# Three edits in the first MLP of an attention-and-two-MLPs kernel: when v is asked for, when tail rows are stored, and the order in which shared fused products are split

## The chip, the cores and the metric

The kernel runs on one core of one Trainium2 chip. The metric is device time in microseconds (us) of one execution. The kernel before takes 1601.68 us, the median of three runs (1598.41 to 1603.44).

## The reference, cut to what matters

A packed attention (32 packing queries p for each of 64 heads) feeds two MLPs. All inputs and outputs are float32.

```python
def sm_attn(qq, kk, vv):
    s = scale * np.matmul(qq, kk.transpose(0, 1, 3, 2))
    s = s - np.max(s, axis=-1, keepdims=True)
    a = np.exp(s)
    a = a / (np.sum(a, axis=-1, keepdims=True) + 1e-09)
    return np.matmul(a, vv)
p_packed = sm_attn(p, k, v)                # batch 8, heads 8, 576 positions, head size 64; p: 32 rows
out = sm_attn(q, p_packed, p_packed)
x = out.transpose(0, 2, 1, 3).reshape(4608, 512)
h = x @ w_in;  x = (h * (1 / (1 + np.exp(-h)))) @ w_out          # first MLP: 512 -> 2048 -> 512
h = x @ w_in2; y = (h * np.clip(h + 3, 0, 6) / 6) @ w_out2       # second MLP, the same sizes
```

## The kernel before

**Tiling.** Sixteen attention groups (batch and four heads each, called n) are worked through in windows that run beside the first MLP. The first MLP has nine blocks j of 512 tokens; blocks 1 to 7 each take the 512 head rows of one batch, block 8 the 64 tail rows of all batches. In each block a loop over 16 slices f of the hidden layer forms `hidden` (lines 829 to 831), applies Silu, splits the result into a high and a low part (`split_g`, lines 844 and 845), and `project` (lines 852 to 854) adds the slice to four PSUM accumulators. Every float32 product is three matmuls over high and low parts: high by high, high by low, low by high. The second MLP follows from about 850 us on and is not touched.

**Fused products.** In blocks 1 to 7 the packed values are multiplied into `w_in` first (`fuse_steps`, lines 617 to 619), so that `hidden` needs only the attention weights. Blocks 2 and 3, 4 and 5, 6 and 7 are mates: one product of 128 rows holds 64 rows for the one and 64 rows for the other (`two`). Each product lies in one PSUM bank; `split` copies its high part on ACT (line 623) and subtracts on DVE for the low part (line 624), for 64 rows at a time when there are mates. There are 48 such shared products: three pairs, four column groups g, two head groups qd, two halves j. The bank comes from a pool of four, which `hidden` also draws on, and it is free again after the last low part. The first mate's tiles are called `fused` in the trace, the second mate's `xf`, `raw`, `xh` and `xl`, by the buffer that they borrow.

**The order.** `window` writes the attention steps of a window in a fixed order with their needs; `Plan` runs them between the MLP's matmuls when their needs have been met for so many steps (`WAIT`, counted in matmul triples). `step_pp` multiplies the attention weights by v (lines 459 to 462); `step_pt` transposes the packed values (line 479). `step_xt` copies a tail result (line 105, tile `xt`), and `flush` stores it (line 562).

**The queue.** Nearly all transfers of the first MLP are issued by SP in program order, and an issue that waits holds all behind it. `load_next` issues the next v, q or k of a list (`uses`), up to three uses ahead. A v load overwrites `vt`, the only buffer for v's tail rows (line 325), so it waits for the matmuls of `step_pp` that read the one before (line 462). On the same queue stand the fused weights' loads `wi` (line 222), `wo` (line 235), and the stores of `Prep` (lines 309 to 311): `Prep` converts the second MLP's weights in one buffer `c`, which POOL (line 293) fills again only after its last store has landed; DVE (lines 296 to 299) then works on it.

Of the kernel before, what the change touches and what calls it, by code (L numbers as in the profile page):

```python
# [18 lines left out]
def tile_pack_attention_two_mlps(ctx: ExitStack, tc, q, k, v, p, w_in1, w_out1, w_in2, w_out2, out):  # L19
# [8 lines left out]
    nc = tc.nc  # L28
# [4 lines left out]
    P = 128  # L33
# [47 lines left out]
    f32 = lambda ap: ap.bitcast(F32)  # L81
# [8 lines left out]
    def bank():  # L90

        pool, tag = (ps_h, "h")
        if early[0]:
            pool, tag = banks[0]
            banks.append(banks.pop(0))
        return pool.tile([P, T], F32, tag=tag, name="abank")
# [4 lines left out]
    def copy(out, in_):  # L101
        (nc.vector.tensor_copy if other[0] else nc.scalar.copy)(out=out, in_=in_)
# [253 lines left out]
    def pair(t, pr):  # L356
        return t[:, 2 * pr:2 * pr + 2, :].rearrange("p h d -> p (h d)")
# [94 lines left out]
    def step_pp(n):  # L452
        vm, vt = [nat.pop(("v", n, j)) for j in range(2)], nat.pop(("v", n))
        a, at_ = st.pop(("a1", n)), st.pop(("a1t", n))
        r = st.pop(("r1", n))
        ps = bank()
        for i in range(NI):
            for h in range(HQ):
                mm(ps[h * NP:(h + 1) * NP, 0:D], lhsT=a[:, i * P + h * NP:i * P + (h + 1) * NP], rhs=vm[h // 2][:, h % 2, i, :],
                   start=i == 0, stop=False)  # L460
        for h in range(HQ):
            mm(ps[h * NP:(h + 1) * NP, 0:D], lhsT=at_[:, h * NP:(h + 1) * NP], rhs=vt[:, h, :], start=False, stop=True)
        pf = at.tile([P, HQ, D], F32, tag="ppf", name="ppf", bufs=3)
        pn = at.tile([P, 1, D], F32, tag="ppn", name="ppn")
        nc.vector.tensor_scalar(out=pn[:, 0, :], in0=ps[:, 0:D], scalar1=r[:, 1:2], scalar2=None, op0=ALU.mult)
        nc.vector.tensor_tensor(out=pf, in0=pn.to_broadcast([P, HQ, D]), in1=mask.to_broadcast([P, HQ, D]), op=ALU.mult)
        st["pp", n] = pf
        if early[0]:
            ph = at.tile([P, HQ, D], F32R, tag="ph", name="ph", bufs=2)
            pl = at.tile([P, HQ, D], F32R, tag="pl", name="pl", bufs=2)  # L470
            copy(out=ph, in_=pf)
            nc.gpsimd.tensor_sub(out=pl, in0=pf, in1=f32(ph))
            st["ps", n] = ph, pl

    def step_pt(n):
        pf = st["pp", n]
        ps = bank()
        for j in range(2):
            nc.tensor.transpose(ps[:, j * P:(j + 1) * P], pair(pf, j), ident)
        t = at.tile([P, 2 * P], F32, tag="ppT", name="ppT", bufs=4)  # L480
        copy_short(out=t, in_=ps[:, 0:2 * P])
        st["ppT", n] = t
# [96 lines left out]
    fused = {}  # L579
# [28 lines left out]
    def fuse_steps(b, g):  # L608

        ms = mates[b]  # L610
        steps = []

        def product(ps, j, qd, first, last):
            lh, ll = [t[:, j * P:(j + 1) * P] for t in st["lp", b, qd]]
            w = have_in[b, g, 2 * qd + j]
            rh, rl = w[:, 0], w[:, 1]
            mm(ps, lhsT=lh, rhs=rh, start=first, stop=False)
            mm(ps, lhsT=lh, rhs=rl, start=False, stop=False)
            mm(ps, lhsT=ll, rhs=rh, start=False, stop=last)

        def split(dst, ps, rows):
            hi, lo = dst[0][rows, :], dst[1][rows, :]
            nc.scalar.copy(out=hi, in_=ps[rows, :])
            nc.vector.tensor_sub(out=lo, in0=ps[rows, :], in1=f32(hi))  # L624

        def one(qd):
            ps = bank()
            for j in range(2):
                product(ps, j, qd, j == 0, j == 1)
            fused[b, g, qd] = fused_tiles(b, g, qd)  # L630
            split(fused[b, g, qd], ps, slice(0, P))
            next_in()
            next_in()

        def two(qd, j):
            ps = bank()
            product(ps, j, qd, True, True)
            for m, bm in enumerate(ms):
                if j == 0:
                    fused[bm, g, qd] = fused_tiles(bm, g, qd)  # L640
                o = m * 64 if j == 0 else (1 - m) * 64
                split(fused[bm, g, qd], ps, slice(o, o + 64))
            next_in()

        for qd in range(QPB):
            if len(ms) == 1:
                steps.append(lambda qd=qd: one(qd))
            else:
                for j in range(2):
                    steps.append(lambda qd=qd, j=j: two(qd, j))  # L650
        return steps
# [9 lines left out]
    uses = []  # L661
# [7 lines left out]
    loaded, used = [0], set()  # L669
    cs = [c for ws in WINDOWS for c, _ in ws if c is not None]  # L670

    def load_next():

        while loaded[0] < len(uses) and (loaded[0] < AHEAD or uses[loaded[0] - AHEAD] in used):
            what, n = uses[loaded[0]]
            loaded[0] += 1
            if what != "k":
                load_tail(n, what)
            for j in range(2):
                load_nat(n, what, j)  # L680

    def use(what, n):
        used.add((what, n))
        load_next()
# [8 lines left out]
    class Plan:  # L693
# [11 lines left out]
        def add(self, key, place, cost, fn, need=(), tile=None, bank=0):  # L705
            self.steps.append((place, key, cost, fn, need, tile, bank))
            self.open.add(key)
# [46 lines left out]
    def window(c, d, b, a):  # L754


        steps = []

        before = ("exps", b, a), ("ends", b, a)

        def add(n, what, cost, fn, *need, tile=None, bank=5):
            if n is not None:
                steps.append(((what, n), cost, fn, need, tile, bank))

        def exps():
            for n, fn in (c, exp1), (d, exp2):
                if n is not None:
                    fn(n)

        def ends():  # L770
            for n, fn in (c, post1), (d, post2):
                if n is not None:
                    fn(n)

        def kpq():
            step_kpq(c, d)
            if c is not None:
                load_p_after(c)

        add(c, "spread", 0, lambda: spread_p(c), ("kpq", b), bank=0)  # L780
        add(c if c is not None else d, "kpq", 3 if c is not None else 1, kpq, ("spread", c), ("st", b), ("zt", a))
        add(b, "t", 2, lambda: step_t(b), before[0], tile=("pp", b))
        add(d, "q0", 0, lambda: step_tr(d, "q", 0), bank=0, tile=("z", d))
        add(b, "tt", 1, lambda: step_tt(b), before[0])
        add(d, "q1", 0, lambda: [step_tr(d, "q", 1), use("q", d)], ("q0", d), bank=0, tile=("z", d))
        ends_block = a is not None and a % QPB == QPB - 1
        if ends_block:
            a = None
        add(a, "u", 0, lambda: [step_u(a), step_ut(a)], before[1], bank=8)
        add(b, "pp", 4, lambda: [step_pp(b), use("v", b)], ("t", b), ("tt", b))  # L790
        add(a, "xt", 1, lambda: step_xt(a), ("u", a))
        add(a, "flush", 0, flush, ("xt", a), bank=0)
        add(b, "pt", 1, lambda: step_pt(b), ("pp", b))
        add(d, "z", 4, lambda: step_z(d), ("pt", d), ("q0", d), ("q1", d), (("u", a), 0), bank=9)
        add(c, "k0", 0, lambda: step_tr(c, "k", 0), (("pp", b), 0), bank=0, tile=("s", c))
        add(d, "zt", 1, lambda: step_zt(d), ("z", d), ("kpq", c if c is not None else d))
        add(c, "k1", 0, lambda: [step_tr(c, "k", 1), use("k", c)], ("k0", c), bank=0, tile=("s", c))
        add(c, "s", 4, lambda: step_s(c), ("k1", c), ("kpq", c), ("tt", b))
        add(c, "st", 1, lambda: step_st(c), ("s", c))
        steps.append((("exps", c, d), 0, exps, (("st", c), ("zt", d)), None, 0))  # L800
        steps.append((("ends", c, d), 0, ends, (("exps", c, d),), None, 0))
        return steps

    WAIT = {"spread": 8, "kpq": 7, "q0": 6, "q1": 6, "k0": 6, "k1": 6, "t": 6, "tt": 5, "pp": 9, "pt": 6, "z": 4, "zt": 10, "s": 4, "st": 7,
            "exps": 18, "ends": 18, "u": 14, "split": 10}
    FIRST = {**WAIT, "ends": 16, "spread": 20, "exps": 14, "pt": 14, "tt": 8, "t": 8, "k1": 8}


# [122 lines left out]
    class Second:  # L931
# [212 lines left out]
        def split(self, s):  # L1144
            if s < FD * S7:
                self.split_hi(s)
                self.split_lo(s)
# [249 lines left out]
    for j in range(NBLK):  # L1397
# [16 lines left out]
        if j in mates:  # L1414
            for g in range(1, NG):
                fs = fuse_steps(j, g)
                lo, hi = [max(0, 18 * g * GF - 24) / (18 * NF) for g in (g - 1, g)]
                for i, fn in enumerate(fs):
                    plan.add(("m", j, g, i), lo + (hi - lo) * 0.7 * (i + 0.5) / len(fs), 6 if len(mates[j]) == 1 else 3, fn, bank=11)
        if j + 1 in mates:  # L1420
            lo = max(at_pp, (18 * 3 * GF - 24) / (18 * NF))
# [86 lines left out]
```

## Time and profile before

| | |
|---|---|
| median of three runs | 1601.68 us |
| the profiled execution, its own time | 1596.71 us |
| its span, first to last instruction | 1594.9 us |
| PE busy, share of the span | 97% |
| DVE, ACT, POOL busy | 65%, 51%, 12% |
| mean granted TensorE clock | 0.988 |

The table is of one profiled execution. PE is the busiest engine by far; the time that can be won is where PE stands idle, or runs at a lower granted clock, so idle time in front of a PE instruction is the first thing to look for, and what ended it the second.

### The profile page before, as it was taken

How to read it: one execution, taken by the hardware profiler on the slowest of the kernel's cores; microseconds unless marked ns; L12 is line 12 of the kernel's file. 1: busy time of each engine (PE TensorE's matmuls, PEld its weight loads, DVE VectorE, ACT ScalarE, POOL GpSimd, SP SyncE). 2: the span in 40 equal slices, each digit the busy share in tenths (PEclk: the TensorE clock that was granted, in tenths of full speed). 3: DMA queues.
4: the chain of work that ended last, by engine and by line, in shares of the span. 5: the costliest groups of instructions: out<-in, count | busy, mean ns of one | idle time of the engine just before them, and what ended most of it. 6: DMA issues, size and time to landing. Idle time of an engine off the chain costs nothing.

```text
span 1594.9 us, 23740 instructions
## 1 busy us (share of the span) xinstructions
PE 1540.4 (97%) x8396; PEld 1334.8 (84%) x8396; DVE 1038.1 (65%) x1765; ACT 809.4 (51%) x1360; POOL 195.0 (12%) x172
## 2 busy tenths in 40 slices
PE   6899998899999999999999999999999999999998
PEld 3667765677777777778888999999999999999998
DVE  5776453665566555663352787787787787787775
ACT  4876544655556445655443453454454454454443
POOL 1433011111111111113132000000000000000000
PEclk9899999999999999999999999999999999999999
DMA  8899784896769776757597888888888978988875
GB/s 216 280 284 285 228 231 113 241 265 187 194 199 235 214 183 194 244 180 226 167 340 240 281 263 263 296 262 264 293 261 263 301 258 263 299 260 262 266 255 174
DMA packets 410198, 388.02 MB, mean 243 GB/s; under 512 B 156256, under 2 KB 282976, under 8 KB 410080
## 3 DMA queue, kind: packets, MB, share of 16 engines
q1 hardware_dynamic: 398704, 371.81, 77.1%
q10 hardware_dynamic: 11376, 14.68, 2.9%
q8 instruction: 68, 1.11, 0.3%
q14 instruction: 50, 0.41, 0.1%
HBM read 324.53 MB, written 61.87 MB: 242 GB/s over the span
## 4 chain that ended last, share of the span: by engine, by line
PE 78%; DVE 6%; ACT 6%; DMA 5%; SPq 2%; issue 2%; POOL 1%; ACTq 0%; DVEq 0%; POOLq 0%
PE b L1098 7%; PE b L1100 7%; PE b L1187 7%; PE b L1188 7%; PE b L1186 7%; PE b L1099 7%; PE acc L852 6%; PE acc L853 6%; PE acc L854 6%; PE hps L829 3%; PE hps L831 3%; PE hps L830 3%; PE abank L495 1%; PE b L1215 1%; DVE fused L624 1%
## 5 line engine op out<-in xcount | busy, mean ns | idle before, releaser
L1186 PE MATMUL b<-ro,ws 128*128 128x384 f32 x672 | 227.5, 339 | 0.0
L1098 PE MATMUL b<-xc,ws 128*128 128x384 f32 x672 | 226.0, 336 | 0.0
L1188 PE MATMUL b<-ro,ws 128*128 128x384 f32 x672 | 225.9, 336 | 0.0
L1187 PE MATMUL b<-ro,ws 128*128 128x384 f32 x672 | 225.9, 336 | 0.0
L1100 PE MATMUL b<-xc,ws 128*128 128x384 f32 x672 | 224.8, 334 | 0.0
L1099 PE MATMUL b<-xc,ws 128*128 128x384 f32 x672 | 224.7, 334 | 0.0
L845 DVE TENSOR_TENSOR gl<-hps,gh 128x512 fp32r<-128x512 f32 x144 | 99.1, 688 | 172.3 <-ACT gh L844 171.8
L1137 ACT CAST ro<-g 128x768 fp32r<-128x768 f32 x168 | 139.2, 837 | 107.2 <-DVE g L1131 36.5
L1142 DVE TENSOR_TENSOR ro<-g,ro 128x768 fp32r<-128x768 f32 x168 | 159.4, 953 | 12.8 <-ACT ro L1137 12.1
L837 ACT ACTIVATE hps<-hps 128x512 f32<-128x512 f32 x144 | 84.0, 584 | 111.9 <-PE hps L831 111.0
L1187 PEld LDWEIGHTS b<-ro,ws 128*128 128x128 f32 x672 | 126.4, 188 | 0.0
L1186 PEld LDWEIGHTS b<-ro,ws 128*128 128x128 f32 x672 | 126.4, 188 | 0.0
L1188 PEld LDWEIGHTS b<-ro,ws 128*128 128x128 f32 x672 | 126.3, 188 | 0.0
L1099 PEld LDWEIGHTS b<-xc,ws 128*128 128x128 f32 x672 | 126.2, 188 | 0.0
L1098 PEld LDWEIGHTS b<-xc,ws 128*128 128x128 f32 x672 | 126.2, 188 | 0.0
L1100 PEld LDWEIGHTS b<-xc,ws 128*128 128x128 f32 x672 | 126.1, 188 | 0.0
L852 PE MATMUL acc<-gh,wr 128*128 128x512 f32 x288 | 118.0, 410 | 0.0
L852 PE MATMUL acc<-gh,wo 128*128 128x512 f32 x288 | 117.1, 407 | 0.0
L853 PE MATMUL acc<-gl,wr 128*128 128x512 f32 x288 | 114.1, 396 | 0.2 <-DVE gl L845 0.2
L854 PE MATMUL acc<-gh,wr 128*128 128x512 f32 x288 | 113.8, 395 | 0.0
L853 PE MATMUL acc<-gl,wo 128*128 128x512 f32 x288 | 113.0, 392 | 0.0
L854 PE MATMUL acc<-gh,wo 128*128 128x512 f32 x288 | 112.7, 391 | 0.0
(261 smaller groups left out, 3003.5 us busy)
## 6 DMA issues: line engine op xcount, KB each, us to landing
ws<-w2in SPq DMA_DIRECT2D x336, 256.0 KB, 4.1
ws<-w2out SPq DMA_DIRECT2D x336, 256.0 KB, 3.6
wi<-w1i SPq DMA_DIRECT2D x80, 512.0 KB, 5.4
wo<-w1o SPq DMA_DIRECT2D x64, 512.0 KB, 5.7
x1d<-x SPq DMA_DIRECT2D x18, 512.0 KB, 5.5
w1i<-win SPq DMA_DIRECT2D x16, 512.0 KB, 7.5
praw<-in_moe_w_in_dram SPq DMA_DIRECT2D x32, 256.0 KB, 5.5
praw<-in_moe_w_out_dram SPq DMA_DIRECT2D x32, 256.0 KB, 4.9
```

Of the source, the lines that this page charges most:

```text
L845: nc.vector.tensor_sub(out=gl, in0=g, in1=f32(gh))
L852: mm(acc[e], lhsT=w[:, 0, s], rhs=gh, start=first, stop=False)
L853: mm(acc[e], lhsT=w[:, 0, s], rhs=gl, start=False, stop=False)
L854: mm(acc[e], lhsT=w[:, 1, s], rhs=gh, start=False, stop=last)
L1098: mm(ps, lhsT=wh, rhs=xs[k][:, 0, c], start=first, stop=False, skip_group_check=True)
L1099: mm(ps, lhsT=wh, rhs=xs[k][:, 1, c], start=False, stop=False, skip_group_check=True)
L1100: mm(ps, lhsT=wl, rhs=xs[k][:, 0, c], start=False, stop=last, skip_group_check=True)
L1137: nc.scalar.copy(out=t[:, 0], in_=self.operand(s))
L1142: nc.vector.tensor_sub(out=t[:, 1], in0=self.operand(s), in1=f32(t[:, 0]))
L1186: mm(acc[i], lhsT=wh, rhs=ro[:, 0, f], start=first, stop=False, skip_group_check=True)
L1187: mm(acc[i], lhsT=wh, rhs=ro[:, 1, f], start=False, stop=False, skip_group_check=True)
L1188: mm(acc[i], lhsT=wl, rhs=ro[:, 0, f], start=False, stop=last, skip_group_check=True)
```

## The change

Three edits. (1) `use("v", b)`, which issues the next v load, moves from `step_pp` to `step_pt`, and `load_next` stops in front of a v as long as an earlier v in the list has not been used. (2) The store of tail rows (`flush`) waits 12 steps behind `step_xt`; before, it had no wait. (3) For a shared product the two high copies come first, then the two low subtractions; before, high, low, high, low.

```diff
-        def split(dst, ps, rows):
-            hi, lo = dst[0][rows, :], dst[1][rows, :]
-            nc.scalar.copy(out=hi, in_=ps[rows, :])
-            nc.vector.tensor_sub(out=lo, in0=ps[rows, :], in1=f32(hi))
+        def split(ps, *parts):
+            for (hi, _), rows in parts:
+                nc.scalar.copy(out=hi[rows, :], in_=ps[rows, :])
+            for (hi, lo), rows in parts:
+                nc.vector.tensor_sub(out=lo[rows, :], in0=ps[rows, :], in1=f32(hi[rows, :]))
...
         def two(qd, j):
             ps = bank()
             product(ps, j, qd, True, True)
+            parts = []
             for m, bm in enumerate(ms):
                 if j == 0:
                     fused[bm, g, qd] = fused_tiles(bm, g, qd)
                 o = m * 64 if j == 0 else (1 - m) * 64
-                split(fused[bm, g, qd], ps, slice(o, o + 64))
+                parts.append((fused[bm, g, qd], slice(o, o + 64)))
+            split(ps, *parts)
             next_in()
...
             what, n = uses[loaded[0]]
+            if what == "v" and any(w == "v" and (w, m) not in used for w, m in uses[:loaded[0]]):
+                return
             loaded[0] += 1
...
-        add(b, "pp", 4, lambda: [step_pp(b), use("v", b)], ("t", b), ("tt", b))
+        add(b, "pp", 4, lambda: step_pp(b), ("t", b), ("tt", b))
...
-        add(b, "pt", 1, lambda: step_pt(b), ("pp", b))
+        add(b, "pt", 1, lambda: [step_pt(b), use("v", b)], ("pp", b))
...
-            "exps": 18, "ends": 18, "u": 14, "split": 10}
+            "exps": 18, "ends": 18, "u": 14, "split": 10, "xt": 12}
```

The order of instructions on PE, DVE, ACT and POOL stays the same; SP's changes, and so do some waits.

**SP in the middle of block 1.** Behind the loads of one v (`vt_2357` and two `nat`) and one k, the queue stood like this (`vt_2461` and two `nat` from `v` are the next v load, `w2in` are the stores of `Prep`, `xtd` the tail store, `wo` a slice of the output weights):

```order
L222 DMA wi_2386<-w1i0_109 128x1024
L222 DMA wi_2388<-w1i1_110 128x1024
L562 DMA xtd_108<-xt_2393 128x2x64
L235 DMA wo_2441<-w1o13_119 128x2x512
L325 DMA vt_2461<-in_v_dram 64x4x64
L335 DMA nat_2463<-in_v_dram 128x2x256
L335 DMA nat_2465<-in_v_dram 128x2x256
L309 DMA w2in0_121<-hi7_2208 128x7x128
L310 DMA w2in0_121<-c8_2207 128x2x128
L311 DMA w2in0_121<-c8_2207 128x5x128
```

and now stands so:

```order
L562 DMA xtd_108<-xt_2377 128x2x64
L325 DMA vt_2406<-in_v_dram 64x4x64
L335 DMA nat_2408<-in_v_dram 128x2x256
L335 DMA nat_2410<-in_v_dram 128x2x256
L342 DMA nat_2412<-in_k_dram 32x16x32 x4
L342 DMA nat_2417<-in_k_dram 32x16x32 x4
L235 DMA wo_2441<-w1o13_119 128x2x512
L309 DMA w2in0_121<-hi7_2208 128x7x128
L310 DMA w2in0_121<-c8_2207 128x2x128
L311 DMA w2in0_121<-c8_2207 128x5x128
L353 DMA pn_2516<-in_p_dram 128x64
L325 DMA kt_2518<-in_k_dram 64x4x64
```

The first v load, now called `vt_2406`, has the two `wi` loads and the tail store ahead of it instead of behind its k loads. The second, which stood ahead of the three stores as `vt_2461`, no longer stands among these rows; it comes behind the `kt` load.

**ACT and DVE at the first shared products (block 2).** On ACT, lines 623, with the semaphores that each copy waits for, before:

```order
L623 CAST fused_2810<-abank_2806 64x512 [waits PE_49]
L623 CAST xf0_2814<-abank_2806 64x512 [waits DVE_49]
L623 CAST fused_2810<-abank_2820 64x512 [waits PE_49]
L623 CAST xf0_2814<-abank_2820 64x512 [waits DVE_49]
L623 CAST fused_2834<-abank_2830 64x512 [waits PE_49]
```

and now:

```order
L623 CAST fused_2810<-abank_2806 64x512 [waits PE_49]
L623 CAST xf0_2812<-abank_2806 64x512
L623 CAST fused_2810<-abank_2820 64x512 [waits PE_49]
L623 CAST xf0_2812<-abank_2820 64x512
L623 CAST fused_2834<-abank_2830 64x512 [waits PE_49]
```

The second copy of a product no longer waits for DVE. On DVE, before:

```order
L624 TENSOR_TENSOR fused_2811<-abank_2806,fused_2810 64x512 [waits Activation_49]
L624 TENSOR_TENSOR xf1_2815<-abank_2806,xf0_2814 64x512 [waits Activation_49]
L624 TENSOR_TENSOR fused_2811<-abank_2820,fused_2810 64x512 [waits Activation_49]
L624 TENSOR_TENSOR xf1_2815<-abank_2820,xf0_2814 64x512 [waits Activation_49]
L624 TENSOR_TENSOR fused_2835<-abank_2830,fused_2834 64x512 [waits Activation_49]
```

and now:

```order
L625 TENSOR_TENSOR fused_2811<-abank_2806,fused_2810 64x512 [waits PE_49,Activation_49]
L625 TENSOR_TENSOR xf1_2813<-abank_2806,xf0_2812 64x512
L625 TENSOR_TENSOR fused_2811<-abank_2820,fused_2810 64x512 [waits PE_49,Activation_49]
L625 TENSOR_TENSOR xf1_2813<-abank_2820,xf0_2812 64x512
L625 TENSOR_TENSOR fused_2835<-abank_2830,fused_2834 64x512 [waits PE_49,Activation_49]
```

The first low part waits once, for the second of the two copies (by the semaphore's value in the program), and the second low part waits for nothing.

## Rows read from the trace of the kernel before

**Rows 1.** The page: the span.
```profile
span 1594.9 us, 23740 instructions
```

**Rows 2.** Windows: stretch, length, busy time of each engine (count), clock, DMA share, GB/s.
```profile
230.00:262.00 32.00, 27.87 (x156) 18.42 (x154) 13.02 (x28) 13.25 (x21) 2.64 (x3) 0.98 0.43 115
260.80:267.63 6.83, 3.04 (x5) 1.24 (x6) 2.52 (x7) 2.11 (x5) 1.43 (x2) 0.50 0.86 213
284.69:288.10 3.41, 3.08 (x7) 2.33 (x8) 2.76 (x5) 2.51 (x5) 0.00 (x0) 0.50 0.98 326
```

**Rows 3.** Waits of SP's queue, whole span: us in total, times, longest.
```profile
SPq L325 <- PE abank L462: 64.6, 12, 18.3
...
SPq L562 <- DVE xt L105: 50.2, 8, 9.4
```

**Rows 4.** Timeline 248 to 268 us: start, length, engine, instruction [idle before, releaser].
```profile
253.86 0.65 SPq L325 DMA_DIRECT2D vt<-in_v_dram  x1
...
256.88 0.95 SPq L311 DMA_DIRECT2D w2in<-c  x1
...
257.62 1.07 PE L407 MATMUL abank<-T,kp 128*64 128x512 f32 x2
...
261.60 1.26 POOL L293 TENSOR_TENSOR c<-pr 128x512 int32<-128x512 int32 x1 [28.72 <-DMA w2in<-c]
...
262.90 0.29 DVE L296 TENSOR_TENSOR c<-c 128x128 f32<-128x128 f32 x1 [6.97 <-POOL c L293]
...
263.84 0.70 DVE L393 STREAM_TRANSPOSE T<-nat 128x512 f32<-128x512 f32 x1
...
264.59 1.97 PE L407 MATMUL abank<-T,kp 128*64 128x512 f32 x2 [5.91 <-DVE T L393]
```

**Rows 5.** Timeline 278 to 287 us, the first shared products of block 2.
```profile
278.69 0.58 ACT L623 CAST fused<-abank 64x512 fp32r<-64x512 f32 x1
...
280.02 0.58 ACT L623 CAST xf<-abank 64x512 fp32r<-64x512 f32 x1 [0.75 <-DVE fused L624]
...
280.51 0.58 ACT L623 CAST fused<-abank 64x512 fp32r<-64x512 f32 x1
280.64 0.69 DVE L624 TENSOR_TENSOR xf<-abank,xf 64x512 fp32r<-64x512 f32 x1 [0.65 <-ACT xf L623]
281.26 0.69 DVE L624 TENSOR_TENSOR fused<-abank,fused 64x512 fp32r<-64x512 f32 x1
...
285.02 0.80 PE L829 MATMUL hps<-a2h,fused 128*128 128x512 f32 x1 [2.52 <-ACT fused L623]
285.13 0.69 DVE L624 TENSOR_TENSOR fused<-abank,fused 64x512 fp32r<-64x512 f32 x1
...
286.04 0.63 PE L831 MATMUL hps<-a2h,fused 128*128 128x512 f32 x1
```

**Rows 6.** Timeline of PE: four later stalls, 290 to 466 us.
```profile
290.69 0.66 PE L557 MATMUL abank<-a2t,ppf 128*128 128x64 f32 x4 [0.51 <-DVE gl L845]
...
295.95 0.47 PE L617 MATMUL abank<-wi,ph 128*128 128x512 f32 x1 [1.07 <-issue]
...
336.78 0.47 PE L617 MATMUL abank<-wi,ph 128*128 128x512 f32 x1 [1.83 <-issue]
...
465.05 0.47 PE L829 MATMUL hps<-a2h,fused 128*128 128x512 f32 x1 [1.01 <-DVE raw L624]
```

**Rows 7.** Timeline 676 to 688 us, the last column group of blocks 6 and 7.
```profile
681.47 0.58 ACT L623 CAST xl<-abank 64x512 fp32r<-64x512 f32 x1 [2.32 <-DVE fused L624]
...
682.09 0.68 DVE L624 TENSOR_TENSOR xl<-abank,xl 64x512 fp32r<-64x512 f32 x1 [0.65 <-ACT xl L623]
...
687.47 0.66 PE L557 MATMUL abank<-a2t,ppf 128*128 128x64 f32 x4 [1.17 <-DVE a2t L535]
```

**Rows 8.** Groups by line, 160 to 880 us: count | busy, mean ns | idle before.
```profile
L393 DVE STREAM_TRANSPOSE T<-nat 128x512 f32<-128x512 f32 x48 | 32.7, 692 | 0.1
...
L623 ACT CAST raw<-abank 64x512 fp32r<-64x512 f32 x12 | 7.0, 582 | 16.3 <-DVE fused L624 16.3
```

More of the change, by code (lines that the diff above doesn't have):

```diff
@@ L630, in one @@
             fused[b, g, qd] = fused_tiles(b, g, qd)
-            split(fused[b, g, qd], ps, slice(0, P))
+            split(ps, (fused[b, g, qd], slice(0, P)))
             next_in()
```

## The prediction

> **What bounds the kernel now.** The table puts PE at 97% busy at a mean granted clock of 0.988. So only two things can be won or lost: time in which PE stands idle, and time at the lower clock. Four views were read, in this order.
>
> First, the timeline of PE, for the stalls that no other PE work fills. The longest one after 160 us is at 264.59: two `step` matmuls (line 407) wait 5.91 us for a DVE transpose [rows 4]. The next is at 285.02, 2.52 us, at the start of block 2, released by a high copy on ACT [rows 5]. Smaller ones follow at 290.69, 295.95, 336.78, 465.05 and 687.47 [rows 6, 7]. Together they are some 14 us.
>
> Second, the windows, for the clock. Over 230 to 262 us PE is busy 27.87 of 32.00 us at 0.98; behind the two long stalls lie 6.83 and 3.41 us at 0.50, which is the lower level, 1.2 GHz. Each begins after PE had stood idle [rows 2]. The same pair of matmuls takes 1.07 us at 257.62 and 1.97 at 264.59 [rows 4].
>
> Third, the waits of SP. A v load waits up to 18.3 us for the matmuls of line 462, and the tail store up to 9.4 us for DVE's line 105 [rows 3]. What stands behind such an issue matters, not the issue itself: the 18.3 us one ends at 253.86, and behind it the stores of `w2in` are issued until 256.88 [rows 4].
>
> Fourth, the groups of lines 623 and 624, for how the shared products run. Four groups of ACT copies, 48 or 49 in all, have 55.3 us of idle time before them, ended by DVE [rows 8]: the second high copy of each product waits for the first low part.
>
> **A. The stall at 264.59.** Followed backwards [rows 4]: T is ready when DVE has done line 393 (starts 263.84); DVE does that after line 296, which begins at 262.90 after 6.97 us of waiting for POOL; POOL's line 293 begins at 261.60, after the last store of `w2in` has landed, having had nothing to do since 261.60 − 28.72 = 232.88; that store was issued at 256.88, behind the v load that was held until 253.86. In the new order that v load stands behind the stores. All that stands ahead of them now stood ahead of the held load before too, and was issued by 253.86 − 18.3 = 235.6. So the stores go out some 18 us earlier, POOL is done before DVE gets there at 262.90 − 6.97 = 255.93, and DVE's work from line 296 on moves forward by 6.97: T is ready at about 264.54 − 6.97 = 257.6. PE finishes the matmuls ahead of this pair at 264.59 − 5.91 = 258.7, so it doesn't wait: **5.9 us**. The clock goes with it: the pair is 0.90 us shorter (1.97 − 1.07), and I take 0.5 for the other matmuls of the slow stretch, in all **1.4**. The bound is half of the 3.04 us that PE was busy there [rows 2], 1.5. A = 7.3, between 0 (the stores stay late) and 7.4.
>
> Here a rule bears on the clock term. The Trainium skill, "TensorE: Matmul & The Clock Gate", section "Terms", estimates the penalty of a throttled stretch as its length times the missing share of the clock. For both slow stretches that estimate is (6.83 + 3.41) × 0.5 = 5.1 us, where the rows give 1.4 here and 0.5 in B. The rows speak against it in the first stretch, where PE was busy 3.04 of 6.83 us and mostly waited for T. By the rule the sum below would be 3.2 us larger.
>
> **B. The start of block 2.** Before, one product takes ACT and DVE 1.93 us in a ring: low, high of the second mate, low. From 281.26 to 285.13 two products pass, 2 × 1.93 [rows 5]. After, the two engines run apart: highs at 0.49 us (280.02 to 280.51), lows at 0.62 (280.64 to 281.26). The first low part waits for both highs, so it starts 0.49 later: the first copy starts at 278.69, the first low started about 0.6 after it and now would at 279.8. The seventh low part (the fourth product's first) then starts at 279.8 + 6 × 0.62 = 283.5 in place of 285.13. Line 831 at 286.04 needs it, so the block starts **1.6** earlier; the wait of 2.52 at 285.02 for the seventh high (278.69 + 6 × 0.49 = 281.6) lies in front of that and goes too, but is not added. ACT is no longer late behind it: I take the stalls of 0.51 and 1.07 [rows 6] as gone, **1.6**. Of the slow clock I take **0.5**: at most half of PE's 3.08 us there is lost, 1.5 [rows 2], but some wait remains and with it perhaps the lower clock. B = 3.7, from 0.5 (only the ring's first products gain) to 5.
>
> **C. Single shared products that PE waits for.** Alone, a product's last low part ends 2.67 us before the change (first high to last low: 0.58 copy, 0.69 low and again both, with handoffs) and about 0.3 earlier after, since two handoffs between the engines become one. At 465.05 [rows 6] and at two places like it I take 0.3 each; at 336.78 (1.83, with ACT late) 0.5. C = 1.4, from 0 to the 2.8 us of the two rows.
>
> **E. The last column group (676 to 688).** ACT's wait of 2.32 us for DVE goes, the second low part no longer waits 0.65 for its high copy, and the chain of ACT behind it runs about 2 us ahead, so that the stall of 1.17 at 687.47 should go [rows 7]: 0.65 + 1.17 = **1.8**, from 0 to 2.3.
>
> **Costs that I put at nothing, and their cover.** (1) The first low part starts 0.49 later in all 48 shared products. Outside block starts PE has `hidden` and `project` of the running block to do, so the delay lies beside them; if PE waited for each, it would be 48 × 0.49 = 23.5. (2) v loads now are asked for one step later and pass up to two `wi` loads and a store. Line 393's transposes, which read k and q behind them on the queue, waited 0.1 us over 48 [rows 8], so loads have slack now; were it gone at one window, I bound it by 3 us, half of the stall that A removes. A v or q load that stops in `load_next` holds only loads, not the stores. (3) The tail store 12 steps later: nothing waits for it, and the wait that SP has at line 562, 50.2 us [rows 3], becomes shorter. That frees loads behind it earlier; I count no gain, because the transposes hardly wait. (4) Before 160 us only the place of loads and stores shifts. I count 0, bounds ±2, the size of one of the smaller stalls.
>
> **Sum.** 7.3 + 3.7 + 1.4 + 1.8 = 14.2 us. The span of 1594.9 [rows 1] becomes 1580.7, the profiled execution's own 1596.71 becomes 1582.5. The median lies 4.97 above that execution; I keep this distance: **1587.5**.
>
> **Rivals.**
> - *The stores stay late.* Some issue ahead of `w2in` still holds SP, xtd or a `wi` whose buffer is busy. For it: SP's waits at 562 reach 9.4 us. Against it: all these were issued by 235.6. It decides when the last store lands so late that POOL's 1.26 us end after 255.93, thus after about 254.6. A is then lost, 7.1 us left: 1594.6.
> - *Nothing is kept.* The time comes back at the next wait: PE reaches the next transposes or fused products earlier and waits there for weights or loads, in a stretch where the DMA share was 0.86 and 0.98 [rows 2]. Against it: the transposes' 0.1 us. About 1600.
> - *Slower: low parts come late.* PE waits for the low parts of shared products, which now start 0.49 later. With all 48 on the path and B, C, E not coming: 23.5 − 7.3 = 16 us more, 1618. It is slower by over 0.3% from (7.3 + 4.8) / 0.49 = 25 of the 48. Against it: before, PE's waits for these were few [rows 5, 6], and only the first low part of two is later, the second is earlier.
> - *The clock gives back more.* Besides the stalls, the slow stretches cost their length times one half, 3.2 us beyond the sum: 1584.3. For it only that PE's queue behind the stall is full at once; this is the rule named under A.
>
> **Chances and range.** About 0.3% (4.8 us) is what a measurement of this kernel can tell from no change. My forecast 0.62, its own range 1582 to 1592; stores late 0.15 (of this a third ends within 0.3%, since 7.1 stands near 4.8); nothing kept 0.09; slower 0.06; the clock 0.08. Faster: 0.62 + 0.10 + 0.08 = 0.80; same 0.14; slower 0.06. The low end of the range, 1579, has all upper bounds (7.4 + 5 + 2.8 + 2.3 + 2 = 19.5, and the clock's 3.2, 22.7 below the median). The high end, 1598, takes in the late stores with 1594.6 and 3 us of late loads.
>
> **What would show it.** Right: in SP's waits the 18.3 us stand behind `w2in`'s stores, POOL's line 293 begins near 250 and not at 261.60, and no stall of some 6 us stands near line 407 at 258; ACT's second copies have no idle time ended by DVE, and the low parts come in pairs 0.62 apart; the two stalls at the start of block 2 and that near 687 are shorter. Wrong: a new PE stall of over 2 us released by a transpose of q, k or v, by a `wi` load, or by line 625 in the middle of a block; or a store that lands after 254.6.

## The result and the profile after

| | before | after |
|---|---|---|
| median | 1601.68 us (1598.41 to 1603.51, 5 runs) | 1582.57 us (1581.67 to 1584.56, 5 runs) |
| ratio, 95% interval | | 0.9886 (0.9871 to 0.9900) |
| span of the profiled execution | 1594.9 us | 1582.7 us |

The changed kernel is 1.1% faster: 19.1 us by the medians, against 14.2 predicted, and inside the stated range. Between the two profiled executions the difference is only 12.2 us. The terms of the sum were read from that profile of before, so they are compared in this pair first; where the rest comes from is a question of its own below. In the changed file the low parts are at line 625, and the lines of the MLP's loop are 5 higher: `hidden` is at 834 to 836.

**The waits of SP.** Its waits for line 462 and line 105 (us in total, times, longest):

```profile
SPq L325 <- PE abank L462: 35.5, 8, 8.2
...
SPq L562 <- DVE xt L105: 9.0, 5, 4.1
```

The wait of 18.3 us is gone from the list, and the tail store's 50.2 us have become 9.0 [rows 3]. SP waits longer at the `wi` loads in their place, for line 619: 97.2 us in all, 59.1 before.

**The place of the longest stall.** Windows (stretch, length, busy time of each engine, clock, DMA share, GB/s), to be held against [rows 2], and the timeline, to be held against [rows 4]:

```profile
230.00:262.00 32.00, 31.18 (x176) 20.91 (x175) 16.70 (x39) 15.16 (x26) 5.69 (x7) 1.00 0.63 156
```

```profile
238.56 1.47 SPq L311 DMA_DIRECT2D w2in<-c  x1
...
249.69 1.29 POOL L293 TENSOR_TENSOR c<-pr 128x512 int32<-128x512 int32 x1 [16.56 <-DVE pr L181]
...
254.07 0.63 SPq L325 DMA_DIRECT2D vt<-in_v_dram  x1
...
256.06 0.25 DVE L296 TENSOR_TENSOR c<-c 128x128 f32<-128x128 f32 x1
...
256.96 0.70 DVE L393 STREAM_TRANSPOSE T<-nat 128x512 f32<-128x512 f32 x1
...
257.83 1.08 PE L407 MATMUL abank<-T,kp 128*64 128x512 f32 x4
258.84 0.50 PE L857 MATMUL acc<-gh,wo 128*128 128x512 f32 x1
```

The matmul behind the two pairs stood here in the kernel before:

```profile
266.49 0.80 PE L852 MATMUL acc<-gh,wo 128*128 128x512 f32 x1
```

Read the changed kernel's timeline from the bottom. The two pairs of `step` matmuls are now one row of four, with nothing between. T starts at 256.96 and not at 263.84; DVE's line 296 has no wait for POOL; POOL starts at 249.69 as soon as DVE's line 181 is done, not when a store has landed; and that store was issued at 238.56, 18.3 us earlier than before. The v load still waits until 254.07, but the stores are no longer behind it; q loads are, and the transposes of line 393 have no wait for them here.

**The start of block 2.** Timeline, to be held against [rows 5]:

```profile
270.54 0.58 ACT L623 CAST fused<-abank 64x512 fp32r<-64x512 f32 x1
271.13 0.58 ACT L623 CAST xf<-abank 64x512 fp32r<-64x512 f32 x1
271.61 0.58 ACT L623 CAST fused<-abank 64x512 fp32r<-64x512 f32 x1
271.74 0.68 DVE L625 TENSOR_TENSOR fused<-abank,fused 64x512 fp32r<-64x512 f32 x1 [1.48 <-ACT xf L623]
...
272.44 0.69 DVE L625 TENSOR_TENSOR xf<-abank,xf 64x512 fp32r<-64x512 f32 x1
...
273.06 0.69 DVE L625 TENSOR_TENSOR fused<-abank,fused 64x512 fp32r<-64x512 f32 x1
...
274.41 0.50 PE L834 MATMUL hps<-a2h,fused 128*128 128x512 f32 x1
...
275.68 0.69 DVE L625 TENSOR_TENSOR fused<-abank,fused 64x512 fp32r<-64x512 f32 x1
...
276.42 0.79 PE L836 MATMUL hps<-a2h,fused 128*128 128x512 f32 x1 [1.28 <-DVE fused L625]
277.01 0.63 PE L834 MATMUL hps<-a2h,fused 128*128 128x512 f32 x1
```

ACT copies without waiting for DVE, and the low parts follow each other. The seventh low part starts 275.68 − 270.54 = 5.14 us after the first copy; before it was 285.13 − 278.69 = 6.44. PE's wait of 2.52 before line 834 is gone, but one of 1.28 for the seventh low part stands one instruction on, and behind it matmuls take 0.63 us, at the lower clock as before: the granted clock from 276.42 to 281.11 is 0.64.

**Later places.** Groups by line over 160 to 860 us, to be held against [rows 8], and PE's timeline, against [rows 6, 7]:

```profile
L623 ACT CAST raw<-abank 64x512 fp32r<-64x512 f32 x12 | 7.0, 581 | 0.2
...
L393 DVE STREAM_TRANSPOSE T<-nat 128x512 f32<-128x512 f32 x48 | 32.9, 693 | 2.0 <-DMA nat<-in_q_dram 1.9
```

```profile
281.11 0.55 PE L557 MATMUL abank<-a2t,ppf 128*128 128x64 f32 x4
...
285.02 0.40 PE L617 MATMUL abank<-wi,ph 128*128 128x512 f32 x1
...
326.27 0.47 PE L617 MATMUL abank<-wi,ph 128*128 128x512 f32 x1 [1.77 <-issue]
...
454.46 0.47 PE L834 MATMUL hps<-a2h,fused 128*128 128x512 f32 x1 [0.94 <-DVE raw L625]
...
529.19 0.66 PE L459 MATMUL abank<-nat,T 128*32 128x64 f32 x32 [1.39 <-ACT T L102]
...
533.17 0.41 PE L479 MATMUL abank<-ident,ppf 128*128 128x128 f32 x2 [0.80 <-DVE ppf L466]
...
672.29 0.47 PE L834 MATMUL hps<-a2h,fused 128*128 128x512 f32 x1 [0.54 <-DVE xl L625]
...
675.13 0.55 PE L557 MATMUL abank<-a2t,ppf 128*128 128x64 f32 x4
```

ACT's idle time before the second copies fell from 16.3 us to 0.2 in one group of four. The stalls at 281, 285 and 675 are gone. Those of a single shared product stand almost whole, 1.77 in place of 1.83 and 0.94 in place of 1.01. And there is one that the first profile of before does not have, 1.39 and 0.80 near 529. Two rows of that profile for comparison, the instruction of 529.19, which has no wait there, and that of 672.29, which waits longer:

```profile
539.99 0.65 PE L459 MATMUL abank<-nat,T 128*32 128x64 f32 x32
...
682.92 0.47 PE L829 MATMUL hps<-a2h,fused 128*128 128x512 f32 x1 [1.22 <-DVE xl L624]
```

In the changed kernel the wait at 529.19 is for ACT, which itself waited for raw weights of `Prep`:

```profile
527.45 0.66 ACT L174 ACTIVATE pr<-praw 128x512 f32<-128x512 f32 x1 [2.39 <-DMA praw<-in_moe_w_in_dram]
```

How far the changed kernel is ahead of that profile, read from the start of the same instruction in both: 0.2 us behind at the first pair of line 407 (257.62, 257.83), 8.2 ahead at the first copy of block 2 (278.69, 270.54), 10.9 at 295.95 (285.02), 11.4 at 299.85 (288.49), 10.5 at 336.78 (326.27), 10.6 at 465.05 (454.46), 12.2 at 510.14 (497.92), 9.9 behind the two waits near 529 (543.02, 533.17), 12.3 at 687.47 (675.13), 12.2 at the end.

### The profile page after: what moved, and what is told of

Same layout as the page of the kernel before. It is cut to its first block, busy times and chain, and to the rows that moved or that the text cites. A ratio compares the mean times of both kernels' runs of the same rounds, so it can differ in the third digit from the quotient of the medians.

```text
span 1582.7 us, 23810 instructions
## 1 busy us (share of the span) xinstructions
PE 1537.4 (97%) x8396; PEld 1334.9 (84%) x8396; DVE 1037.9 (66%) x1765; ACT 810.8 (51%) x1360; POOL 194.4 (12%) x172
## 4 chain that ended last, share of the span: by engine, by line
PE 84%; DMA 4%; ACT 3%; DVE 3%; SPq 2%; issue 1%; POOL 1%; POOLq 0%; ACTq 0%; DVEq 0%
PE b L1103 7%; PE b L1105 7%; PE b L1191 7%; PE b L1193 7%; PE b L1104 7%; PE b L1192 7%; PE acc L857 7%; PE acc L858 7%; PE acc L859 7%; PE hps L834 4%; PE hps L836 4%; PE hps L835 4%; PE abank L407 1%; PE abank L495 1%; PE b L1220 1%
```

## The experiments

Two explanations stood against each other at each gain. Theory: the long stall hangs on the stores of `w2in` behind the held v load (edit 1), the rest on the order of copies (edit 3), and edit 2 gives nothing. Rivals: the tail store or the loads make the gain; or the losses near 529 are what edit 1 costs. Ratios are to the kernel before on the same chip, with 95% intervals; the changed kernel has 0.9886 (0.9871 to 0.9900).

**One edit at a time.** e1 has edit (3) alone, e2 edit (1), e3 edit (2); their diffs are the parts of the change.

> The kernel before with edit (3) alone: two high copies, then two low parts. If the gains at the block starts and in the last column group belong to this edit: the stall of 5.9 us at 264.59 stays whole, PE gains about 3 us between 278 and 300, 0.1 to 0.2 at each single product that it waits for, and about 2.5 us between 676 and 690; in all 5.5 us less, ratio 0.9965, and no new loss of 2.4 us near 540. If those gains came from the order of the loads instead (ACT and DVE late only because weights were late): nothing, ratio 1.000. If the first low part, half a copy later, costs at products in mid-block: slower than before, up to 1.01.

Measured: 0.9963 (0.9949 to 0.9977). PE's timeline of e1 at the second pair of line 407, at the start of block 2, near 540, and twice in the last column group:

```profile
265.19 1.97 PE L407 MATMUL abank<-T,kp 128*64 128x512 f32 x2 [5.56 <-DVE T L393]
...
285.88 0.50 PE L834 MATMUL hps<-a2h,fused 128*128 128x512 f32 x1 [1.28 <-DVE fused L625]
...
541.92 0.65 PE L459 MATMUL abank<-nat,T 128*32 128x64 f32 x32 [1.57 <-ACT T L102]
...
685.61 0.47 PE L832 MATMUL hps<-a2h,fused 128*128 128x512 f32 x1 [0.54 <-DVE xl L625]
...
688.46 0.55 PE L557 MATMUL abank<-a2t,ppf 128*128 128x64 f32 x4
```

The long stall stands, the gains at the block start and at 688 come: they are the split's. But near 540 this kernel loses time too, against the expectation, though it doesn't have edit (1).

> The kernel before with edit (1) alone: v asked for in step_pt, and no v load while an earlier v is unused. If the stall at 264.59 hangs on the v load that holds SP: it goes, about 8 us with the slow clock behind it. If the loss of about 2.4 us near 540 in the changed kernel is the price of this edit (v behind a wi load that waits for its buffer, and so the raw weights late): it stands here too; net 5.5 us less, ratio 0.9965. If the tail store ahead of the v load holds SP as long without edit (2): the stores of w2in stay late, less than 2 us gained, ratio 0.999 to 1.001.

Measured: 0.9958 (0.9943 to 0.9973). The stall is gone with this edit alone, although SP still waits for the tail rows (66.5 us at line 562 for `xt`); the loss near 540 stands:

```profile
257.86 1.08 PE L407 MATMUL abank<-T,kp 128*64 128x512 f32 x4
...
537.25 0.65 PE L459 MATMUL abank<-nat,T 128*32 128x64 f32 x32 [1.07 <-ACT T L102]
```

> The kernel before with edit (2) alone: the tail store 12 steps later. By the prediction: the 50.2 us that SP waits for line 105 fall below 15, and the time doesn't move, 0 with 1 us to either side, ratio 0.999 to 1.001. If SP's waits for the tail rows hold loads that PE needs: 2 to 5 us less, ratio 0.997 to 0.999, with the stall at 264.59 shorter.

Measured: 0.9996 (0.9985 to 1.0006), no change, with SP's waits at line 562 for `xt` at 12.6 us in place of 50.2. The tail-store rival falls: taking 37.6 us of these waits away gained nothing.

**The stores alone.** e4 leaves all of the kernel before as it is and takes the three stores behind the held load off SP:

```diff
+                store = nc.scalar if u == 1 else nc.sync
-                nc.sync.dma_start(out=to[:, :, h * P:(h + 1) * P], in_=hi)
+                store.dma_start(out=to[:, :, h * P:(h + 1) * P], in_=hi)
...
```

> The kernel before, with the three w2in stores that stood behind the held v load (the second unit of Prep) issued by ACT in place of SP; all else as before, the v load still holds SP for some 18 us. If the late stores are what makes PE wait at 264.59: the stall goes, with the slow clock behind it, 8 us less, ratio 0.995, though SP's queue is as late as before. If the loads behind the v load are the cause, or POOL waits for something else: the stall stays, ratio 1.000; if ACT pays for the issues (some 0.5 us each), up to 2 us come back.

Measured: 0.9945 (0.9927 to 0.9964), 8.8 us. The store issued by ACT, POOL, and PE:

```profile
243.39 0.92 ACTq L312 DMA_DIRECT2D w2in<-c  x1
...
249.72 1.29 POOL L293 TENSOR_TENSOR c<-pr 128x512 int32<-128x512 int32 x1 [16.58 <-DMA xtd<-xt]
...
257.87 1.08 PE L408 MATMUL abank<-T,kp 128*64 128x512 f32 x4
```

POOL starts at the same time as in the changed kernel and the stall is gone, with v asked for where it always was and its load issued at 254.11, as late as before. The chain store, POOL, DVE, T is thereby shown as the cause.

**The kernel before, and the changed one, once more.** Both for second profiles; e11 is unchanged `after`.

> The kernel before once more, for a second profile. Near 337 and near 540 the kernels with one edit each lost some 2 to 4 us and 2 us against the first profile of before. If these losses belong to the executions (a store of w2in and raw weights that land later in some): here at least one of the two stands as well, and the span is nearer to 1600 than to 1594.9. If they belong to the edits: neither stands here, and the span is 1595 within 1 us.

One execution took 1602.51 us, with a span of 1600.7. Two places:

```profile
332.00:345.00 13.00, 10.51 (x76) 7.61 (x75) 7.71 (x19) 5.88 (x11) 3.23 (x3) 0.87 0.99 238
```

```profile
505.35 1.29 POOL L293 TENSOR_TENSOR c<-pr 128x512 int32<-128x512 int32 x1 [18.44 <-DMA w2in<-c]
...
505.55 1.12 DVE L520 TENSOR_SCALAR s2s<-s2s 128x18 f32<-128x18 f32 x1
...
510.73 0.65 PE L459 MATMUL abank<-nat,T 128*32 128x64 f32 x32 [1.39 <-DVE a1Tt L105]
```

The same program is 5.8 us longer here than in its first profile. It ran on a chip where the median of before is 1603.29, so up to 1.6 us of this can be the chip's. The loss is in small pieces: 1.4 us stand before 230, 1.0 come from slow matmuls behind the stall of line 407, 2.4 near 337 and 0.9 at 505, and the last two show how. In 332 to 345 us the clock is at 0.87, behind two waits of PE, 0.37 at 336 and 0.30 at 337, in place of which the first profile has 0.10 at most. At 505 POOL's line 293, which again starts when a store of `w2in` has landed, falls on a small DVE operation that takes 1.12 us beside it, where it took 0.18 in the first profile, and PE waits 1.39 in place of 0.45. Near 540 nothing is lost in this execution, as nothing was in the first profile. So the first profile was a quick execution: its 1596.71 us lie below all 50 executions of before that were timed beside the runs (1596.91 to 1606.98). The loss near 337 comes and goes in one and the same program. That the landing of stores decides it is a reading that fits at 505 and isn't shown for 337.

> The changed kernel again, for a second profile and a second interval. If its first profile had a chance loss of 2.4 us near 529 (raw weights landing 2 us late, as also in kernels with one edit): near 529 the loss differs by over 1 us here. If the loss is the price of v behind a wi load that waits: it stands here too, within 0.5 us. Ratio to before 0.987 to 0.990.

Measured: 0.9891 (0.9873 to 0.9908), with a span of 1581.5. The window that takes in the place of 337, which the changed kernel reaches some 10 us earlier:

```profile
300.00:345.00 45.00, 42.69 (x227) 30.48 (x225) 29.00 (x55) 25.93 (x44) 3.51 (x3) 1.00 0.79 220
```

PE's wait of 1.39 at line 459 near 529 is 0.26 here, that of 0.80 at line 479 stands again. So the size of this loss is chance, but that there is one may be a price of the change; e12 takes it up. The window is at full clock, as it is in the first profile of after. Between the two second profiles the change is worth 1600.7 − 1581.5 = 19.2 us, close to the 19.1 between the medians, though the two come from different chips (medians of before 1603.29 and 1601.91).

**The place of the request, and edit (2) on top.** e5 is the changed kernel with the request back in `step_pp`, e10 is it without edit (2):

```diff
-        add(b, "pp", 4, lambda: step_pp(b), ("t", b), ("tt", b))
+        add(b, "pp", 4, lambda: [step_pp(b), use("v", b)], ("t", b), ("tt", b))
...
-        add(b, "pt", 1, lambda: [step_pt(b), use("v", b)], ("pp", b))
+        add(b, "pt", 1, lambda: step_pt(b), ("pp", b))
```

> The changed kernel, but v is asked for in step_pp as before; the stop in front of a v while an earlier v is unused stays. If that stop alone takes the held v load off the stores of w2in: same as the changed kernel, ratio to before 0.9885, no stall near 258. If the place of the request counts: either the v loads hold SP for line 462 again and the stall of about 6 us returns (ratio 0.993), or they no longer stand behind a wi load that waits, and the raw weights that came 2 us late near 529 come in time (2 to 3 us more gained, ratio 0.987).

Measured: 0.9876 (0.9856 to 0.9895). No stall near 258, no difference from the changed kernel that the intervals separate: of edit (1) the stop in `load_next` does the work, the move of the request none that shows in the time. In its profile the raw weights near 529 land in time and PE doesn't wait there.

> The changed kernel without edit (2): the tail store has no wait again. If edit (2) is worth nothing, as alone (0.9996): the same as the changed kernel, ratio to before 0.9885, and the stall at 258 stays away, since the tail store ahead of the v load is issued early enough. If the three edits gain more together (0.9886 measured) than alone (0.9963, 0.9958 and 0.9996, product 0.9917) because the tail store would hold the stores of w2in and the raw weights: 3 to 5 us slower than the changed kernel, ratio 0.991 to 0.992.

Measured: 0.9902 (0.9887 to 0.9917), beside 0.9891 for the changed kernel (e11), timed along with it. Not separated: the medians differ by 2.0 us, and the intervals leave room for nothing as well as for the 3 to 5 us of the second expectation. What edit (2) is worth on top of the others stays open.

**Spacing of the copies.** e7 reverses the halves of every second product:

```diff
-            split(ps, *parts)
+            split(ps, *(parts if j == 0 else parts[::-1]))
```

> The changed kernel with the two halves of every second shared product (j = 1) in reversed order, so that the half of the rows now changes between products too, not only within one. It tells why the second copy of a product starts 0.59 after the first, and the first of the next 0.48 after the second, where the prediction took 0.49 for all. If the spacing comes from reading the same PSUM bank twice in a row: 0.59 within a product and 0.48 between, as before. If it comes from a change of rows 0-63 to 64-127: 0.59 within and between. Time within 0.3% of the changed kernel by both.

Measured: 0.9895 (0.9868 to 0.9923). ACT at the start of block 2 (x2 is two copies in a row, here the last of one product and the first of the next):

```profile
270.69 0.58 ACT L623 CAST fused<-abank 64x512 fp32r<-64x512 f32 x1
271.28 1.19 ACT L623 CAST xf<-abank 64x512 fp32r<-64x512 f32 x2
272.48 1.18 ACT L623 CAST fused<-abank 64x512 fp32r<-64x512 f32 x2
273.67 1.19 ACT L623 CAST xf<-abank 64x512 fp32r<-64x512 f32 x2
```

Now all copies are 0.59 to 0.60 apart, within a product and between products. It is the change between rows 0-63 and 64-127 that costs 0.11 us, not the bank. A copy lasts 0.58: where the rows change, the next one starts when the one before has ended, and where they don't, it starts 0.10 before that end.

**Raw weights and stores.** Three attempts at what is left. e8 issues all stores of `Prep` from ACT. e12 asks for raw weights earlier, e13 adds e5's edit to e12:

```diff
+                if u + 1 < len(self.units):
+                    self.load(u + 1)
                 conv_begin(key, self.room)
...
-                if u + 1 < len(self.units):
-                    self.load(u + 1)
                 yield
```

> The changed kernel with all stores of Prep issued by ACT in place of SP. If late stores of w2in (POOL waits for them once more near 318, DVE 1.0 us for POOL) and SP's load are what is left to win: POOL's line 293 no longer waits for w2in, 1 to 4 us less than the changed kernel, ratio to before 0.986 to 0.988. If ACT pays for 96 issues of 0.4 to 0.9 us: as much lost again or more, ratio 0.989 to 0.993.

Measured: 1.0081 (1.0061 to 1.0100), slower than before, some 31 us over the changed kernel by the ratios, far beyond what either theory said. Two of its PE stalls:

```profile
295.17 0.77 PE L617 MATMUL abank<-wi,ph 128*128 128x512 f32 x1 [4.72 <-DMA wi<-w1i]
```

```profile
550.18 0.66 ACT L174 ACTIVATE pr<-praw 128x512 f32<-128x512 f32 x1 [10.05 <-DMA praw<-in_moe_w_in_dram]
...
551.91 1.08 PE L459 MATMUL abank<-nat,T 128*32 128x64 f32 x32 [8.87 <-ACT T L102]
```

The loads on SP's queue, `wi` and raw weights, land late here. Against the changed kernel PE loses 4.9 us at the first of these places, 7.5 at the second and 3.4 near 603, where ACT again waits for raw weights: about half of the 31 us. The rest is spread over smaller losses that weren't traced, so ACT's issues aren't ruled out for it, and why the loads land late with the stores on another queue wasn't tried.

> The changed kernel, with each half slice of raw weights asked for at the start of the unit before (its buffer is free by then), some 4 steps of Prep earlier. If late raw weights make ACT wait, and PE behind it, near 529 (2.4 us) and in some executions elsewhere: these losses go, 2 to 4 us less than the changed kernel, ratio to before 0.986. If the earlier issues push back the loads behind them on SP as much: no change, 0.9885, or slower, with a transpose waiting for q or k.

Measured: 0.9893 (0.9874 to 0.9911). The places near 529 are without a wait:

```profile
527.81 0.65 PE L459 MATMUL abank<-nat,T 128*32 128x64 f32 x32
...
530.83 0.38 PE L479 MATMUL abank<-ident,ppf 128*128 128x128 f32 x2
```

Over all fourteen profiles PE waits at this line 459 in just those eight in which ACT's line 174 waits for raw weights (1.3 to 10.1 us: e1, e2, e4, e7, e8, e10 and both of the changed kernel). Both of before, e3, e5, e12 and e13 have neither wait. So late raw weights do make that loss. It isn't all chance either: before and e3 never have it, and of the nine profiles with edit (1) or (3) or with stores on ACT, and raw weights asked for at the old place, eight do. In the first profiles raw weights were issued 6.6 us before ACT took them (530.66, 537.23), and in the changed kernel 4.2 us before ACT was free to (520.90, 525.06); the last landed 6.2 and 6.5 us after that issue. But the time is that of the changed kernel (0.9891), so what is gained there is too small to show or is given back elsewhere.

> As the last, and v asked for in step_pp again with the stop kept (that kernel alone: 0.9876 with an interval of 0.9856 to 0.9895). If both take load off the place near 529: the gains don't add, ratio 0.986. If the two act at different places: 0.985 or below.

Measured: 0.9870 (0.9853 to 0.9888), median 1580.32 us: the lowest of all, 3.0 us under the changed kernel timed along with it (1583.32), with intervals that overlap. It beats before, but not the changed kernel by anything that these runs tell.

## Why the prediction was right, and where it was not

**A, 7.3 predicted, 8.4 measured** (0.2 behind to 8.2 ahead), above the bound of 7.4. Each link held: store, POOL, DVE, T, and no wait at 258.7. e2 and e4 show it alone, and gain the same 8.4 us between the same instructions. The clock term was the small part and too low. From the first pair's start to the matmul behind the second it took 8.87 us (257.62 to 266.49) and takes 1.01 (257.83 to 258.84). Less the wait of 5.91 that is 1.95, where the prediction had 0.90 from the lengths of two rows. The 0.5 behind the pair held: three matmuls took 1.32 us there (266.49 to 267.81) and take 0.82. Together 8.4 − 5.9 = 2.5 us for the clock and the rest, against 1.4 from the rows. The whole-stretch estimate of the Trainium skill ("TensorE: Matmul & The Clock Gate", "Terms"), 6.83 × 0.5 = 3.4 us for this stretch, lies above the 2.5.

**B, 3.7 predicted, 2.8 measured** (8.2 to 10.9). The ring opened as forecast. The seventh low part came 1.3 us earlier and not 1.6, for the reason given under C, and the lower clock was not avoided: 1.28 us of waiting at 276.42 and matmuls of 0.63 us remain. The smaller stalls of 0.51 and 1.07 are gone. In e1 the same place, with the same 1.28, gained 4.0 us, and there the clock stayed at 1.00 (285 to 290 us): how much of B comes depends on the clock of the execution.

**C, 1.4 predicted, 0.4 measured**: the stall of 336.78 shrank by 0.06, that of 465.05 by 0.07, and two like them at 510.14 and 639.06 by 0.16 and 0.07 (1.01 to 0.85, 0.73 to 0.66). This is the term that failed. It priced the handoff that falls away at 0.3. Behind that stood the spacings of 0.49 and 0.62 used in B, which in [rows 5] are those from one product to the next; in the kernel before, the two copies of one product never follow each other, so no row gave theirs. Within a product the copies are 0.59 apart and the lows 0.70 (271.13 − 270.54, 272.44 − 271.74). The chain from first copy to last low is then 0.59 + 0.58 + 0.70 + 0.69 and a handoff of 0.03, 2.59 us in place of 2.67. The lower end of the bound, 0, was near.

**E, 1.8 predicted, 2.4 measured.** At the group itself 682.92 to 687.47 took 4.55 us before and 672.29 to 675.13 takes 2.84: 1.7, and the wait in front of it fell from 1.22 to 0.54, 0.7 more: just above the bound of 2.3. e1 has the same rows.

**The costs put at nothing.** The first low part, 0.5 us later, made PE wait longer at the start of block 2 only (1.28 at 276.42); the slower rival would have shown in e1. Transposes wait 2.0 us in place of 0.1 over 48. e3 shows edit (2) alone at 0. A cost that the prediction didn't name is that of raw weights, which land late near 529: 2.4 us in this pair of profiles, 1.3 in the second profile.

**What no term had.** The four terms came to 8.4 + 2.8 + 0.4 + 2.4 = 14.0 us at their places, beside 14.2 predicted; that the sum is so close is luck, since A and E were too low by 1.7 us and B and C too high by 1.9. Beside them the order of copies also gave 0.4 us at 299.85 and most of some 1.5 between 465 and 515 (the same places gain in e1), and against these stand 0.9 lost before 336.78 and the 2.4 near 529.

**The step that failed outright is the last one: "The median lies 4.97 above that execution; I keep this distance."** The profiled execution of before was a quick one; e9 is 5.8 us longer with the same program. The profiled execution of after, 1584.56 us, was a slow one, 1.99 above its median. So the distance of 12.15 between the two executions becomes 12.15 + 4.97 + 1.99 = 19.11 between the medians. Against the first pair of profiles the sum was 2 us too high, 14.2 for 12.2; against the medians 5 us too low. Nothing in the sum stood for the losses that come and go.

**What stays open.** The three edits alone multiply to 0.9963 × 0.9958 × 0.9996 = 0.9917, together they give 0.9886, some 5 us more, about as much as the intervals allow. A reading that fits is that the loss of clock near 337 happens less in the changed kernel. Over 300 to 345 us the clock is at 1.00 in five of the eight profiles with edits (1) and (3) (both of the changed kernel, e5, e8, e10) and at 0.96 in three (e7, e12, e13); of the six without both it is at 1.00 in the first profile of before alone, and at 0.92 or 0.96 in five. Where it falls, 1.5 to 2.7 us are lost. So few profiles can't show how often, and what makes it fall is open: the short waits of e9 at 336 and 337 stand in the changed kernel too (0.37 and 0.30), without the fall, and e7 has the fall without them.

## What to carry to other kernels

When an engine waits for a store, look at what stands ahead of the store on its queue: here a load that waited for its buffer held a store, and the store held three engines. The cure was not to ask for the load while the one before was still unused. Moving the three held stores to another queue cured the stall too; moving all of them there cost 31 us, about half of it in waits for loads. And profile the kernel before more than once: a sum made against one execution carries that execution's luck, here 5.0 us of a gain of 19.1.

## What the runs showed of the hardware

- A copy of 64 rows on ACT starts 0.48 us after the one before it if both work on the same rows, and 0.59 to 0.60 if the rows change between 0-63 and 64-127; it lasts 0.58 in both cases, so that with a change of rows it starts at the end of the one before. For DVE's subtraction, which lasts 0.69, it is 0.61 to 0.62 and 0.69 to 0.73. The bank makes no difference (e7).
- A DVE operation on a 128x18 tile took 1.12 us beside POOL's line 293, and 0.18 without it (e9, 505 us). The same operation took 0.30 in e4 and 0.57 in e12 where it began later beside line 293; in all three it ended 0.03 us after POOL's instruction did. It takes 0.18 where it begins in the last 0.05 us of it (after).
